# Transposing pairs of bf16 columns as 4-byte elements, and reading every second value as weights

## Chip, core and metric

The kernel runs on one core of one Trainium2 chip. The metric is device time in microseconds (us); lower is better. A run's time is that of the whole execution; the profile's span runs from the first to the last recorded instruction.

## What is computed

The reference is the forward pass and all gradients of two branches that share a layer-normalised input: segment-wise attention with a recurrent memory (A), and an MLP with a squared ReLU (B).

```python
xn = _layernorm(x)
out = x + A(xn, mem0, Wq, Wk, Wv, Wo) + B(xn, w1, b1, w2, b2)

# A: 64 segments of 32 rows, one after the other
mem = mem0                                  # 8 rows
for s in range(n_seg):
    h = concatenate([mem, xs], axis=1)      # 8 + 32 rows of 512
    q, k, v = h @ Wq, h @ Wk, h @ Wv        # 32 heads of 128
    p = softmax(where(mask, q @ k.T * scale, -1e9))
    o = (p @ v) @ Wo
    mem = o[:, :8]                          # goes into the next segment
    outs.append(o[:, 8:])
```

x is 2048 x 512 in bf16, F of the MLP is 1792. The outputs are the result and the gradients of x, mem0, Wq, Wk, Wv, Wo, w1, b1, w2 and b2. The memory makes the 64 segments a chain, forward in one direction and backward in the other.

## The kernel before

**Stages.** First the MLP and the layer norm (to 228 us of the span); then the 64 forward segments (to about 1290); a short turn of the weights (to about 1352); the 64 backward segments (to about 2516); and last the weight gradients of the attention as long runs of 512-column products (to the end). Four segments make a block of 128 rows. A step is one segment.

**Layout of a segment.** The 32 heads are laid out as 8 groups (index i) of 4 heads (index j, "JQ = 4"). In the natural layout (qN, oN, dN and so on, 128 x 1024) the partitions are 4 heads times 32 rows, and the columns are 8 groups times 128 features of a head. Products with Wo or with the turned Wq, Wk, Wv need the transposed layout (OT, dT, LT, qLT): features on the partitions, 32 rows as the columns of each weight. TensorE reads these as stationary weights of 128 x 32, four at a time in four column strips of the array, while the weight matrix streams past.

**The transposes.** `sq_T` (line 395) makes this layout without PSUM: for each half (four groups) one instruction of the VectorE (DVE) transposes 32 x 32 blocks. A block takes every fourth column of a head's 128 features (c is the column modulo 4), so that the 32 features a of one c end up on the partitions of that head's strip; the strip j and the index c together say which weight rows a product needs. Wo is loaded, and Wq, Wk, Wv are turned, in an order of rows to match (`turn`, `turn_o`). `sq_T` is called for oN to OT in each forward step (line 944), for oLN to qLT in `l_attn` (once a block), for dN2, dN1 and dN0 to dT2, dT1 and dT0 in each backward step (in `part`), and for dLN to LT0, LT1 and LT2 in `l_post` (once a block): 640 instructions in all.

**Who reads them.** `wo_part` (line 807) multiplies OT or qLT with Wo: 128 products of 128 columns, in four parts of 32; parts 0 and 1 need the first half of OT, parts 2 and 3 the second. `dh_part` (line 1110) multiplies dT or LT with the turned weights: 32 products of 512 columns, in four parts of 8; the three of a step add up in one PSUM bank.

**A forward step (`chain`, line 907).** Products for q and k; transposes on TensorE; scores; softmax on DVE and ScalarE (ACT); products for v; two DVE transposes of the probabilities (lines 938 and 939); products p v ("ps_o"); eviction to oN by ACT or DVE; `sq_T`; `wo_part` ("ps_RA"); the first eight rows go into the next step's input ("ps_mem", line 951).

**A backward step (`chain`, line 1236).** Products gO and their transposes; dP; the backward of the softmax, four DVE instructions one after the other (lines 1101 to 1106, result in the tile maskA); then three parts, each with a block-diagonal product ("ps_d"), an eviction to dN, `sq_T` and `dh_part`: part 2 needs only gO and P, parts 1 and 0 the softmax. After the last product of part 0 two evictions to R_A (half by ACT, half by DVE), small products ("ps_gm") and a copy into PA (line 1287) end the step.

**Work beside the chain.** Once a block, `l_proj` and `l_attn` (forward) and `l_pre` and `l_post` (backward) treat the block's 32 memory rows; the MLP's weight gradients ("ps_dw", `dw_unit`) fill the forward stage. In `l_pre` the tile dLN is computed (ps_dqL) and stored to S_GNL in DRAM; `l_post` of the block before reloads such a stored tile into the same dLN, transposes it to LT0, then evicts two more products (ps_dL) into dLN, each of which is transposed (LT1, LT2) and stored.

**What sets the order.** Every operation is given to a planner (`_Plan`) with an estimated cost per engine, what it reads and writes, and a priority. `run` simulates the engines with these costs and picks, step by step, the operation that can start first, or one of higher rank (its longest path to the end, from the same costs) that is about to be ready; a change of the shape of TensorE's tiles costs 2.0 us of rank in the backward stage (KEEP). An eviction may go to DVE or ACT, whichever ends it first by the estimates. The order found this way is the program's order on each engine, on the SP queue (loads and stores) and on the POOL queue. A cost changes nothing else: on the chip each engine takes its instructions in that order, and each waits for its own inputs.

Of the kernel before, what the change touches and what calls it, by code (L numbers as in the profile page):

```python
# [16 lines left out]
F32 = mybir.dt.float32  # L17
# [12 lines left out]
def pe(cost, shape):  # L30
    x = _PE(PE=cost)
    x.shape = shape
    return x
# [154 lines left out]
def kernel(  # L188
# [27 lines left out]
    nc = tc.nc  # L216
# [31 lines left out]
    JQ = 4  # L248
# [76 lines left out]
    def part_of(t, x, n):  # L325
        return t[x // n][:, x % n, :]
# [7 lines left out]
    def flat(t):  # L334
        return t[:].rearrange("p i e -> p (i e)")

    EV_F = {"DVE": 0.70, "ACT": 0.59}
    EV_B = {"DVE": 0.44, "ACT": 0.59}
    T_DMA = 0.42

    class Stage:
# [53 lines left out]
        def sq_T(self, src, sk, dst, dk, prio):  # L395

            for half in range(2):
                x = slice(4 * half, 4 * half + 4)
                self.plan.add({"DVE": 0.70}, lambda e, x=x: nc.vector.transpose(  # L399
                    dst[:, x, :, :], src[:, x, :].rearrange("p i (a c) -> p i c a", c=JQ)),  # L400
                    [(sk, half)], [(dk, half)], prio)

        def evict(self, out_f, bk, in_f, W, prio, cost, R=()):
# [3 lines left out]
        def proj(self, kind, nm, win, wkeys, Wt, col0, dst, prio):  # L407
            for half in range(2):
                bk = self.bank(kind, [P, 512], F32, "ps_" + nm)
                for dq in range(2):  # L410
                    def mm(e, half=half, dq=dq, bk=bk):
                        for dc in (2 * dq, 2 * dq + 1):
# [7 lines left out]
                self.evict(lambda half=half: dst[1][:, 4 * half:4 * half + 4, :].rearrange("p i e -> p (i e)"),  # L420
                           bk, lambda bk=bk: bk()[:], [(dst[0], half)], prio, EV_F)

# [18 lines left out]
        def diag(self, kind, nm, terms, rkeys, dst, prio):  # L441
            n = len(terms)
            for half in range(2):
                bk = self.bank(kind, [P, 512], F32, "ps_" + nm)

                def mm(e, half=half, bk=bk):
                    for k in range(4):
                        i = 4 * half + k
                        for x, (lf, rf, m) in enumerate(terms):
# [7 lines left out]
                self.evict(lambda half=half: dst[1][:, 4 * half:4 * half + 4, :].rearrange("p i e -> p (i e)"),  # L457
                           bk, lambda bk=bk: bk()[:], [(dst[0], half)], prio, EV_F)

# [21 lines left out]
    def wtf(t, h):  # L481
        return Wqkv[t][:, :, h * P:(h + 1) * P]
# [27 lines left out]
    with tc.tile_pool(name="p0", bufs=1) as p0, \  # L510
# [184 lines left out]
        for g in range(NRB):  # L695
            if g == 0:
# [12 lines left out]
                bk = sg.bank("B", [P, DC, RB], BF16, "ps_gT")  # L709
# [25 lines left out]
            if g < 6:  # L735
                for h in range(2):
                    x = 2 * g + h
                    t, dc = x // DC, x % DC
# [16 lines left out]
    with tc.tile_pool(name="fw", bufs=1) as fw, \  # L755
# [51 lines left out]
        def wo_part(kind, nm, OTt, ok, prio):  # L807
            bk = sg.bank(kind, [P, P], F32, "ps_R" + nm)
            for q in range(4):
                def mm(e, q=q):  # L810
                    for i in (2 * q, 2 * q + 1):
                        for j in range(JQ):
                            for jd in range(DC):
                                nc.tensor.matmul(  # L814
                                    bk()[32 * jd:32 * (jd + 1), :], lhsT=OTt[:, i, j, :],
                                    rhs=Wo[:, JQ * i + j, jd * P:(jd + 1) * P],
                                    start=(i == 0 and j == 0), stop=(i == NI - 1 and j == JQ - 1),
                                    tile_position=(0, 32 * jd),
                                )
                A(pe(0.54, "w"), mm, [(ok, q // 2), "WB"], [bk.key], prio)  # L820
            return bk
# [172 lines left out]
        def dw_unit(which, u):  # L994
# [16 lines left out]
            for x in range(2):  # L1011
                fc = 2 * u + x
                sg.evict(lambda: wt[:], bks[x], lambda x=x: bks[x]()[:], ["wt"] + ([("dw", u + FC // 2 * which)] if x else []), 1, EV_F)
                if which == 0:
# [39 lines left out]
    if True:  # L1054
# [55 lines left out]
        def dh_part(kind, nm, XT, xk, t, first, last, prio, bk=None):  # L1110
            if bk is None:
                bk = sg.bank(kind, [P, D], F32, "ps_dR" + nm)
            for q in range(4):
                def mm(e, q=q):
                    for i in (2 * q, 2 * q + 1):
                        for j in range(JQ):
                            nc.tensor.matmul(bk()[32 * j:32 * (j + 1), :], lhsT=XT[:, i, j, :],  # L1117
                                             rhs=wtf(t, JQ * i + j), start=(first and i == 0),
                                             stop=(last and i == NI - 1), tile_position=(0, 32 * j))
                A(pe(0.435, "w"), mm, [(xk, q // 2)] + [((t, "WT"), g) for g in range(4 * q, 4 * q + 4)], [bk.key], prio)  # L1120
            return bk
# [42 lines left out]
        def l_post(b):  # L1164
# [8 lines left out]
            for t, ly, lx, lk, big, pad, dst, dk, bn, pn in (parts if b else parts[::-1]):  # L1173
# [37 lines left out]
                for half in range(2):  # L1211
                    sg.evict(lambda half=half: dLN[:, 4 * half:4 * half + 4, :].rearrange("p i e -> p (i e)"), bks[half],
                             lambda half=half, bks=bks: bks[half]()[:], [("dLN", half)], 1, EV_F)
                sg.dma(lambda t=t: part_of(S_GNL[t], b, BPC), lambda: flat(dLN), both("dLN"), [("S_GNL", t, b)])
# [3 lines left out]
            for x, (t, L_) in enumerate(order):  # L1218
                bR = dh_part("f" if b else LKIND, "L", L_, "LT%d" % t, t, x == 0, x == 2, 1, bR)
            sg.evict(lambda: flat(btL), bR, lambda: bR()[:], ["btL"], 1, EV_F)  # L1220
            sg.dma(lambda: S_RL[b], lambda: flat(btL), ["btL"], [], cost=T_DMA + (b == 0), eng="SP" if b else "POOL")
# [14 lines left out]
        def chain(s):  # L1236
# [52 lines left out]
            else:  # L1289
                bm = sg.bank("c", [M, D], F32, "ps_dm0")  # L1290
                A(pe(0.9, "f"), lambda e: nc.tensor.matmul(bm()[:], lhsT=sel8[:], rhs=R_A[:], start=True, stop=True),
                  [("R_A", 0), ("R_A", 1)], [bm.key], 0)
                sg.evict(lambda: gNat[0:M, :], bm, lambda: bm()[:], ["gNat"], 0, EV_F)
                sg.dma(lambda: out2flat[:, :], lambda: gNat[0:M, :], ["gNat"], [])
# [25 lines left out]
        for b in range(TC - 1, -1, -1):  # L1320
            for v in range(SPB - 1, -1, -1):
                s = b * SPB + v
# [23 lines left out]
        for x in range(NRC // BPC):  # L1346
            c0 = (3, 2, 1, 0, 4)[x] * BPC
            src = S_HNA if c0 < TC else S_HNL
# [16 lines left out]
    with tc.tile_pool(name="p5b", bufs=1) as p5b, tc.tile_pool(name="p5e", bufs=1) as cs1, \  # L1365
# [60 lines left out]
        with tc.manual_schedule():  # L1426
            load_gn(0)
            for x in range(4 * JQ):
                t, j = (2, 1, 0, 3)[x // JQ], x % JQ
# [71 lines left out]
```

## Time and profile before

| | us |
|---|---|
| median of 3 runs (lowest to highest) | 3122.26 (3120.48 to 3124.76) |
| span of the profiled execution | 3097.7 |
| forward stage, 228 to 1290 us | 1062 |
| backward stage, 1352 to 2516 us | 1164 |
| TensorE (PE) busy in the span | 2792.6 |
| DVE busy in the span | 1538.8 |
| ACT busy in the span | 933.7 |

The page shows the span of the profiled execution; the launch around it is not in the span. A group of instructions is named by its line, engine and operation, output and input, with its count, busy time, the mean of one in ns, and the idle time of the engine ahead of it with what ended it. PEld is TensorE's loading of weights, which overlaps its products; "issue" is idle time in which nothing that the profile shows was waited for. Helpers have one line for all their calls: 318 is every eviction by ACT, 316 by DVE, 399 every `sq_T`, 361 most DMAs.

### The profile page before, as it was taken

The page shows a single profiled execution, that of the slowest core. Times are in us where ns is not written, and L with a number is a line of the kernel's source. Part 1 is how long each engine was busy: PE and PEld are TensorE (multiplying, and loading weights), DVE is VectorE, ACT ScalarE, POOL GpSimd, SP SyncE. Part 2 cuts the span into 40 slices and gives each one's busy share as a digit, 9 for nine tenths or more (in the row PEclk, how much of TensorE's full clock was granted, in tenths as well). Part 3 has the DMA queues.
Part 4 walks back from the last instruction along what each step waited for, and adds up shares of the span by engine and source line. Part 5 has one row for each costly group of instructions (what it writes and reads, how often), then busy time and mean ns, then how long its engine had stood idle before and what let it go on. Part 6 is the DMA issues. An engine that isn't in the chain of part 4 may idle for free.

```text
span 3097.7 us, 138545 instructions
## 1 busy us (share of the span) xinstructions
PE 2792.6 (90%) x62681; PEld 1629.5 (53%) x62847; DVE 1538.8 (50%) x3390; ACT 933.7 (30%) x1809; POOL 260.8 (8%) x434
## 2 busy tenths in 40 slices
PE   8998889898889898798888898889899889999999
PEld 6664555555555555564555555555555544444444
DVE  5544545555545455575555565565556521233322
ACT  4323434433434344342233333333333310000000
POOL 1110000000000000100000000000000001121111
PEclk9999999999999999999999999999999989999999
DMA  6647655566665563357677777777777669789861
GB/s 205 217 155 212 173 157 171 160 174 167 163 160 153 162 168 125 98 143 195 184 208 193 204 204 202 207 200 213 208 214 206 201 238 351 223 253 280 253 184 45
DMA packets 554918, 590.54 MB, mean 191 GB/s; under 512 B 250197, under 2 KB 355110, under 8 KB 552150
## 3 DMA queue, kind: packets, MB, share of 16 engines
q1 hardware_dynamic: 538758, 527.06, 59.8%
q0 software_dynamic: 15568, 54.61, 5.3%
q8 instruction: 491, 8.04, 1.2%
q14 instruction: 101, 0.83, 0.1%
HBM read 283.32 MB, written 262.68 MB: 176 GB/s over the span
## 4 chain that ended last, share of the span: by engine, by line
PE 67%; issue 10%; DVE 8%; DMA 8%; SPq 3%; ACT 2%; POOL 1%; ACTq 0%; POOLq 0%; DVEq 0%
PE ps_gw L1448 11%; PE ps_dRA L1117 9%; PE ps_d L451 6%; PE ps_RA L814 4%; PE ps_q L415 4%; PE ps_k L415 3%; PE ps_h L609 3%; PE ps_gO L415 3%; SPq L361 3%; PE ps_dRL L1117 3%; PE ps_v L415 2%; PE ps_dw L1009 2%; PE ps_gm L1284 2%; PE ps_o L451 2%; PE ps_gxb L637 2%
## 5 line engine op out<-in xcount | busy, mean ns | idle before, releaser
L1117 PE MATMUL ps_dRA<-WA,dT 128*32 128x512 bf16 x6144 | 376.6, 385 | 12.9 <-issue 10.4
L1448 PE MATMUL ps_gw<-WA,WB 128*128 128x512 bf16 x1505 | 330.7, 379 | 2.2 <-DVE gwo L316 0.6
L415 PEld LDWEIGHTS <-PA 128*32 128x32 bf16 x8192 | 207.5, 98 | 235.7 <-issue 29.8
L1448 PEld LDWEIGHTS <-WB 128*128 128x128 bf16 x1896 | 185.4, 98 | 225.0 <-issue 1.9
L399 DVE STREAM_TRANSPOSE dT<-dN 128x512 bf16<-128x512 bf16 x384 | 255.5, 692 | 90.7 <-ACT dN L318 89.4
L318 ACT CAST dN<-ps_d 128x512 bf16<-128x512 f32 x356 | 198.8, 588 | 292.0 <-PE ps_d L451 257.2
L1117 PEld LDWEIGHTS <-dT 128*32 128x32 bf16 x6144 | 158.0, 97 | 169.5 <-issue 26.5
L316 DVE CAST gwo<-ps_gw 128x512 bf16<-128x512 f32 x64 | 39.7, 683 | 399.5 <-PE ps_gw L1448 268.2
L814 PE MATMUL ps_RA<-WB,OT 128*32 128x128 bf16 x8192 | 139.3, 223 | 58.2 <-issue 41.9
L318 ACT CAST gwo<-ps_gw 128x512 bf16<-128x512 f32 x64 | 32.9, 599 | 515.3 <-PE ps_gw L1448 357.8
L316 DVE CAST kN<-ps_k 128x512 bf16<-128x512 f32 x117 | 80.9, 691 | 191.4 <-PE ps_k L415 188.4
L415 PE MATMUL ps_q<-WA,PA 128*32 128x512 bf16 x2048 | 160.9, 383 | 9.5 <-DVE PA L951 5.5
L814 PEld LDWEIGHTS <-OT 128*32 128x32 bf16 x8192 | 123.4, 99 | 78.9 <-issue 48.2
L415 PE MATMUL ps_k<-WA,PA 128*32 128x512 bf16 x2048 | 159.7, 380 | 1.6 <-issue 1.3
L451 PEld LDWEIGHTS <-PB 32*32 32x32 bf16 x8192 | 120.4, 93 | 72.6 <-issue 33.9
L415 PE MATMUL ps_gO<-WB,PA 128*32 128x512 bf16 x2048 | 139.5, 418 | 15.1 <-DVE PA L1287 14.9
L1227 POOL COPY bVT<-VR 128x1024 bf16<-128x1024 bf16 x64 | 66.6, 1041 | 959.1 <-PE ps_dP L1249 880.8
L318 ACT CAST qN<-ps_q 128x512 bf16<-128x512 f32 x119 | 69.6, 585 | 197.8 <-PE ps_q L415 194.7
L415 PE MATMUL ps_v<-WA,PA 128*32 128x512 bf16 x2048 | 128.1, 378 | 0.0
L1009 PE MATMUL ps_dw<-sx,anT 128*128 128x512 bf16 x358 | 108.0, 385 | 10.3 <-DMA sx<-in_grad_out_dram 6.6
L399 DVE STREAM_TRANSPOSE OT<-oN 128x512 bf16<-128x512 bf16 x128 | 83.8, 691 | 59.6 <-ACT oN L318 59.0
L1117 PE MATMUL ps_dRL<-WA,LT 128*32 128x512 bf16 x1536 | 111.2, 395 | 1.4 <-issue 1.0
(298 smaller groups left out, 4778.2 us busy)
## 6 DMA issues: line engine op xcount, KB each, us to landing
S_GN<-dN SPq DMA_DIRECT2D x192, 256.0 KB
WA<-S_GN SPq DMA_DIRECT2D x160, 256.0 KB
S_Q<-qN SPq DMA_DIRECT2D x64, 256.0 KB
S_K<-kN SPq DMA_DIRECT2D x64, 256.0 KB
S_V<-vN SPq DMA_DIRECT2D x64, 256.0 KB
S_ON<-oN SPq DMA_DIRECT2D x64, 256.0 KB
bqN<-S_Q SPq DMA_DIRECT2D x64, 256.0 KB
bkN<-S_K SPq DMA_DIRECT2D x64, 256.0 KB
```

Of the source, the lines that this page charges most:

```text
L316: nc.vector.tensor_copy(out, in_)
L318: nc.scalar.copy(out, in_)
L361: self.plan.add({eng: cost}, lambda e: q.dma_start(out_f(), in_f()), R, W, prio, lat)
L399: self.plan.add({"DVE": 0.70}, lambda e, x=x: nc.vector.transpose(dst[:, x, :, :], src[:, x, :].rearrange("p i (a c) -> p i c a", c=JQ)), ...
L415: nc.tensor.matmul(bk()[32 * j:32 * (j + 1), :], lhsT=win(dc), rhs=Wt(dc, c0), start=(dc == 0), stop=(dc == DC - 1), tile_position=(0, 32 ...
L451: nc.tensor.matmul(bk()[32 * j:32 * j + m, k * P:(k + 1) * P], lhsT=lf(j, i), rhs=rf(j, i), start=(k == 0 and x == 0), stop=(x == n - 1), ...
L609: nc.tensor.matmul(bk()[:, x, :], lhsT=Wt[:, dc, fc * P:(fc + 1) * P], rhs=In[:, dc, :], start=(dc == 0), stop=(dc == DC - 1), skip_group_ ...
L814: nc.tensor.matmul(bk()[32 * jd:32 * (jd + 1), :], lhsT=OTt[:, i, j, :], rhs=Wo[:, JQ * i + j, jd * P:(jd + 1) * P], start=(i == 0 and j = ...
L1009: nc.tensor.matmul(bks[x]()[:], lhsT=anT[x][:, c, :], rhs=sx[z][:], start=(c == 0), stop=(c == TC - 1))
L1117: nc.tensor.matmul(bk()[32 * j:32 * (j + 1), :], lhsT=XT[:, i, j, :], rhs=wtf(t, JQ * i + j), start=(first and i == 0), stop=(last and i = ...
L1227: A({"POOL": 1.0}, lambda e: nc.gpsimd.tensor_copy(VT[:, :, :, M:KA].rearrange("p i j r -> p (i j) r"), VR[:].rearrange("p i j r -> p (i j ...
L1448: nc.tensor.matmul(bks[n]()[:], lhsT=HNc[:, rc, dc * P:(dc + 1) * P], rhs=gns[y][:, hf * 512:(hf + 1) * 512], start=(y == 0), stop=(y == N ...
```

## The change

`sq_T` reads its source and writes its destination as 4-byte elements, each of which is two neighbouring bf16 columns. One instruction then handles 256 elements a partition instead of 512: 8 blocks of 32 x 32 instead of 16. A block takes every second pair of columns (u is the pair modulo 2). In the destination, a row's two values s = 0 and 1 of a pair now lie side by side, so the weight for column class k = 2u + s is every second value of a run of 64; the new helper `tq` gives that view, and `wo_part` and `dh_part` use it for their weights. The class k holds the same features as c did. The planner's cost for the transpose goes from 0.70 to 0.42.

```diff
+    def tq(t, i, k):
+        return t[:, i, :, :].rearrange("p c r -> p (c r)").rearrange("p (u r s) -> p u s r", u=2, s=2)[:, k // 2, k % 2, :]
+
@@ sq_T
-                self.plan.add({"DVE": 0.70}, lambda e, x=x: nc.vector.transpose(
-                    dst[:, x, :, :], src[:, x, :].rearrange("p i (a c) -> p i c a", c=JQ)),
+                self.plan.add({"DVE": 0.42}, lambda e, x=x: nc.vector.transpose(
+                    dst[:, x, :, :].rearrange("p i c r -> p (i c r)").bitcast(F32).rearrange("p (i u r) -> p i u r", u=2, r=32),
+                    src[:, x, :].rearrange("p i e -> p (i e)").bitcast(F32).rearrange("p (i a u) -> p i u a", a=32, u=2)),
                     [(sk, half)], [(dk, half)], prio)
@@ wo_part
-                                    bk()[32 * jd:32 * (jd + 1), :], lhsT=OTt[:, i, j, :],
+                                    bk()[32 * jd:32 * (jd + 1), :], lhsT=tq(OTt, i, j),
@@ dh_part
-                            nc.tensor.matmul(bk()[32 * j:32 * (j + 1), :], lhsT=XT[:, i, j, :],
+                            nc.tensor.matmul(bk()[32 * j:32 * (j + 1), :], lhsT=tq(XT, i, j),
```

## The prediction

> **What bounds the kernel now.** I read the page first: one line of busy times, then the groups of the line that the change rewrites.
>
> ```profile
> PE 2792.6 (90%) x62681; PEld 1629.5 (53%) x62847; DVE 1538.8 (50%) x3390; ACT 933.7 (30%) x1809; POOL 260.8 (8%) x434
> ...
> L399 DVE STREAM_TRANSPOSE dT<-dN 128x512 bf16<-128x512 bf16 x384 | 255.5, 692 | 90.7 <-ACT dN L318 89.4
> ...
> L399 DVE STREAM_TRANSPOSE OT<-oN 128x512 bf16<-128x512 bf16 x128 | 83.8, 691 | 59.6 <-ACT oN L318 59.0
> ```
>
> TensorE (PE) is busy 90%, VectorE (DVE) half. Line 399 runs 384 + 128 + 96 (LT) + 32 (qLT) = 640 times at 0.69 us. An engine half idle gains nothing by itself; what counts is who waits. So next the view of line 399 alone:
>
> ```profile
> who waited for it (us, times):
>   PEld L814: 32.0, 49
>   ACT dLN L318: 20.8, 11
>   PE ps_RA L814: 15.5, 19
>   POOL PB L1139: 15.1, 2
>   PEld L1117: 9.4, 35
> ```
>
> TensorE's weight loads wait for these transposes in 49 of the 64 forward steps (L814), on average 0.65 us; in the backward steps (L1117) hardly at all. The chain of waits agrees: its pieces on line 399, added up over the whole chain, are 23.5 us OT, 16.8 dT and 6.1 LT, 46.4 in all. The busy time by stretch gives the stages: forward 228 to 1290 us with 134 us of idle PE, backward 1352 to 2516 with 128.
>
> **The price of the parts.** No row shows a transpose of 4-byte elements. The nearest rows handle as many elements as the new instruction (256 a partition), in 2 bytes:
>
> ```profile
> L938 DVE STREAM_TRANSPOSE PB<-P 128x256 bf16<-128x256 bf16 x64 | 28.0, 437 | 0.0
> ...
> L939 DVE STREAM_TRANSPOSE PB<-PLp 128x256 bf16<-128x256 bf16 x64 | 25.7, 402 | 0.0
> ```
>
> I take 0.42, between the two, so 0.27 us less each and 173 us less DVE work. Bounds: 0.69, if a 4-byte element takes two passes (no gain), and 0.28, the quickest 256-element DVE row (L614, 285 ns).
>
> The weights with a step of 2: products of 512 columns run four at a time, 245 ns a group (L1117: 376.6 us for 6144), and hide four loads each. In wo_part (L814, 128 columns) the timeline shows 96 loads in 1.39 us, the pace of the products. The nearest row is the turning of WA (L312), which reads weights with a step of 4: 115 ns against 98 for the contiguous kN, and eight loads in 0.51 us against 0.45. Of these 0.06 us, 0.015 is latency; the rest is 5 ns per 128 columns, or 1.3 ns per load of 32. Times 10,240 loads of L814 that is 13 us at most. Eight of those transposes take 0.61 us against 0.62 for contiguous WB, so the pace of the products does not change: I take 0. [...]
>
> **Forward.** Of the 64 steps, the 16 with l_attn hold two transposes more and stall on "issue" before L814 (60.3 us in all, gaps where nothing is waited for); I count nothing there. In the other 48 OT's first half comes 0.27 us sooner: 13 us; the chain's share says 23.5 x 0.27/0.69 = 9. I take **-10** (bounds 0 and -18). Late next: ACT's eviction of oN, which the transposes themselves wait for (59.0 us).
>
> **Backward: the order changes.** The planner sorts instructions by estimated cost, and 0.70 became 0.42. The instruction order of the built changed kernel, against that of the one before, shows what follows. Before, nearly every step runs the products for dN0 in one piece ahead of the last dh_part products. In 30 of 62 steps of the changed kernel (3 before) dN0's first half comes early and its second half only after half of dT0's products, so that eviction, transpose and the last products stand in a row; and in 15 of them (2 before) nothing lies between dP and the products that wait for the whole softmax. The steps come in pairs, two of every block of four. DVE's other work, ACT's evictions, the SP queue's loads and the l_post products move with them: the reload of dLN now falls due a step later, and ACT's eviction of the next dLN, which waits for the store of the one before, stands ahead of ACT's R_A, the end of the step.
>
> One block of the kernel before happens to have this very order: the steps from 1478 us (a step runs from one copy of ps_gm into PA, L1287, to the next). Busy time by stretch, first its four steps, then four of a regular block:
>
> ```profile
> 1478.48:1498.05 19.57, 16.32 (x528) 10.35 (x532) 12.19 (x24) 5.35 (x10) 1.38 (x2) 0.91 0.45 136
> 1498.05:1521.33 23.28, 17.17 (x484) 10.81 (x476) 13.72 (x26) 5.45 (x10) 1.68 (x3) 0.90 0.97 256
> 1521.33:1540.43 19.10, 19.10 (x444) 9.95 (x446) 8.68 (x19) 4.28 (x8) 1.38 (x2) 0.85 0.55 166
> 1540.43:1555.70 15.27, 14.72 (x412) 8.43 (x412) 8.67 (x18) 4.86 (x9) 1.38 (x2) 1.00 0.88 197
> 2083.16:2103.03 19.87, 15.97 (x516) 10.01 (x516) 12.37 (x24) 6.99 (x13) 1.68 (x3) 1.00 0.67 175
> 2103.03:2121.64 18.61, 17.43 (x452) 11.12 (x456) 10.68 (x23) 5.87 (x11) 1.38 (x2) 0.91 0.82 250
> 2121.64:2137.70 16.06, 16.06 (x436) 9.15 (x435) 8.70 (x19) 4.95 (x9) 1.38 (x2) 1.00 0.78 207
> 2137.70:2154.00 16.30, 15.62 (x472) 9.46 (x464) 10.48 (x22) 5.53 (x10) 1.38 (x2) 1.00 0.70 208
> ```
>
> After the length come busy PE, PEld, DVE, ACT and POOL, then the granted clock. The odd block takes 77.25 us; the twelve regular blocks from 1571 to 2440 us average 72.4: **+4.85**. It also shows why:
>
> ```profile
> 1506.25 0.23 PE L451 MATMUL ps_d<-bqN,maskA 32*32 32x128 bf16 x4 [2.21 <-DVE maskA L1106]
> ...
> 1518.81 0.58 ACT L318 CAST dLN<-ps_dL 128x512 bf16<-128x512 f32 x1 [3.69 <-DMA S_GNL<-dLN]
> ```
>
> PE idles 2.2 us for the softmax, ACT 3.7 us for a store ahead of R_A, and the granted clock falls to 0.85 to 0.91 in three steps. The regular block loses clock in one; there DVE idles 3.0 us at 2100.8 for dLN's reload.
>
> What the shorter transposes give back in such a block, walked through its timeline: first odd step 0.2 (two of dT2 ahead of PB) + 0.28 (PE waits 0.55 for dT0) = 0.5; second 0.6 (five shorter transposes ahead of dLN let its store start some 1.2 earlier, but ACT now evicts both halves behind it, which takes 1.1 instead of 0.6); 0.3 each in the other two: 1.7. So 14 further blocks cost 14 x (4.85 - 1.7) = **+44**. The bounds: +18 more, as the odd block holds 1.3 us less work than a full one (16 gL products at 54 ns, eight transposes at 56), and -41 if its third step keeps the full clock (0.15 of 19.1 us = 2.9 a block).
>
> MLP, weight gradients and launch are untouched: 0. The sum: 3122 - 10 + 44 = **3156**, say 3155. The profiled span is 3097.7; 24.6 us of the median lie around it and stay.
>
> **Rivals.**
> (1) Faster: the odd block was slow by accident, and only the 46.4 us that line 399 holds of the chain shrink by 0.27/0.69: -18, 3104. For it: a single block, with DMA busy 97% in its second step. Against: the 2.2 us gaps follow from the order.
> (2) Faster, by the clock: were the dips not to come, the odd block would be shorter by 0.09 x 16.3 + 0.01 x 17.2 + 0.15 x 19.1 = 4.5 us, nearly the whole +4.85; 14 x (0.35 - 1.7) - 10 = -29, 3093. The trace speaks against it: the first odd step shows 0.91 with no gap above 2.2 us. The Trainium skill, TensorE: Matmul & The Clock Gate, Part 1, states that the clock halves only after an idle window of about 3.4 us; by that rule this case holds, and the row 0.91 disagrees.
> (3) The 4-byte transpose takes 0.69 like the old one: the change doesn't do what it says, the new order stays: 14 x 4.85 = +68, 3190.
> (4) Stepped weights cost 1.3 ns a load on L814: +13 on the forecast, 3168.
> (5) Gain and order cancel: 3122.
>
> **How the numbers follow.** Forecast 0.51 (alone 3130 to 3185), (1) 0.17, (2) 0.07, (3) 0.09, (4) 0.06, (5) 0.10. Measurement tells some 0.2% (6 us) from no change: faster 0.24, same 0.10, slower 0.66. The range 3100 to 3190 leaves out (2) and the upper half of (3).
>
> **What would show it.** Line 399 at 0.40 to 0.44 us (else 3). PEld's wait at L814 for OT near 20 instead of 32 us. Backward blocks near 75.5 us instead of 72.4, with PE gaps of 2 us before ps_d<-maskA, ACT dLN waiting for S_GNL, and granted clock under 0.95 in two or three steps of four. Backward blocks at 71 would make me wrong, by (1) or (2). L814's loads above 16 ns apiece would show (4).

## The result and the profile after

| | before | changed |
|---|---|---|
| median of 4 runs, us (lowest to highest) | 3121.37 (3100.27 to 3124.76) | 3161.7 (3148.22 to 3168.89) |
| ratio to before, 95% interval | | 1.0152 [1.0121, 1.0182] |
| span of the profiled execution, us | 3097.7 | 3161.9 |
| backward steps, first to last copy of ps_gm into PA, us | 1132.1 | 1185.5 |
| forward steps, first to last copy of ps_mem into PA, us | 1038.0 | 1054.4 |
| mean of 13 whole blocks (the second to the fourteenth of the backward stage), us | 72.62 | 77.26 |

The changed kernel is slower: by 40 us (1.3%) by the medians, by 1.52%, some 47 us, by the ratio of the runs. The 64 us between the two spans are 53.4 in the backward steps, 16.4 in the forward steps and -6 in the rest. The 16 in the forward steps do not belong to the change: the kernels below that have the forward order of before take 1045 to 1054 us there, too (e1, e4, e7, e8), and on a third chip the same order takes 1023.5 us (e12), so these steps vary by some 30 us between runs and chips. The profile of before is of a quick execution: the changed kernel's profiled run (3163.7) lies 1.8 us above its span, and by the same margin a span of 3097.7 belongs to a run of about 3099.5 us, 22 under the median and near the fourth of its runs (3100.27).

First the page and the groups of the changed kernel: busy times, then line 402, which is line 399 of before.

```profile
PE 2830.5 (90%) x62669; PEld 1647.3 (52%) x62847; DVE 1427.5 (45%) x3459; ACT 898.7 (28%) x1740; POOL 260.7 (8%) x434
...
L402 DVE STREAM_TRANSPOSE dT<-dN 128x256 f32<-128x256 f32 x384 | 163.0, 434 | 170.4 <-ACT dN L318 166.6
...
L402 DVE STREAM_TRANSPOSE OT<-oN 128x256 f32<-128x256 f32 x128 | 57.3, 448 | 52.9 <-ACT oN L318 49.8
```

The instruction does what was promised: 0.43 to 0.45 us instead of 0.69. DVE is busy 111 us less, and the kernel is slower.

Next the waits of TensorE within the backward stage (us in total, times, longest), of before and of the changed kernel, both from 1384 to 2515 us of the span (the changed kernel's last 55 us of backward steps are not in it):

```profile
PE ps_d L451 <- DVE maskA L1106: 17.1, 24, 2.2
...
PE ps_dL L1205 <- DMA ys<-S_PL: 9.7, 12, 1.7
```

```profile
PE ps_d L455 <- DVE maskA L1110: 54.5, 28, 3.0
PE ps_dL L1209 <- DMA ys<-S_PL: 36.4, 27, 2.6
```

Two waits grew: 37 us more for the softmax, which the prediction named, and 27 us more for ys, a load of `l_post`, which it did not. (In e1 below, which has the order of before, the wait for ys is 17.6 us, so a part of the 27 varies between runs.) Then busy time by stretch, for four steps of one changed block and the fourth step of the next (length; busy PE, PEld, DVE, ACT, POOL; granted clock; share of DMA busy; GB/s):

```profile
1532.59:1551.13 18.54, 16.27 (x436) 9.35 (x436) 7.35 (x18) 4.28 (x8) 1.38 (x2) 1.00 0.68 196
1551.13:1566.70 15.57, 15.54 (x428) 8.91 (x424) 7.80 (x20) 5.54 (x10) 1.38 (x2) 1.00 0.79 194
1566.70:1585.49 18.79, 15.96 (x536) 10.04 (x537) 11.80 (x26) 5.25 (x10) 1.38 (x2) 1.00 0.48 143
1585.49:1609.87 24.38, 19.04 (x492) 10.60 (x484) 10.15 (x25) 5.84 (x11) 1.63 (x3) 0.86 0.95 238
...
1660.06:1686.85 26.79, 20.12 (x492) 11.66 (x484) 10.34 (x24) 6.33 (x12) 1.88 (x3) 0.80 0.98 263
```

One step of four holds nearly the whole loss. On average over the fifteen blocks it takes 24.3 us at a DMA share of 0.94; the longest of the four in before takes 20.4 us, and no place there averages over 0.79 DMA. The other three together take 52.5 us, and 52.3 in before. The timeline of TensorE in such a step (1660.06 to 1686.85 us) shows what stands there:

```profile
1662.04 0.62 PE L1209 MATMUL ps_dL<-xs,ys 128*32 128x128 bf16 x32
...
1667.71 0.23 PE L455 MATMUL ps_d<-bqN,maskA 32*32 32x128 bf16 x4 [2.98 <-DVE maskA L1110]
...
1676.14 0.39 PE L1198 MATMUL ps_dL<-gLN,bPLL 32*32 32x128 bf16 x16
1676.46 0.23 PE L1209 MATMUL ps_dL<-xs,ys 128*32 128x128 bf16 x1
1678.26 0.23 PE L1209 MATMUL ps_dL<-xs,ys 128*32 128x128 bf16 x1 [1.57 <-DMA ys<-S_PL]
1680.54 0.82 PE L1209 MATMUL ps_dL<-xs,ys 128*32 128x128 bf16 x14 [2.05 <-DMA ys<-S_PL]
...
1682.23 1.92 PE L1121 MATMUL ps_dRA<-WA,dT 128*32 128x512 bf16 x16
```

`l_post` has two rounds of ps_dL that use the same tiles xs and ys: t = 1, then t = 2, with eight loads for each. In the changed kernel both rounds fall into this one step. The first ends at 1662.7; only then can the tiles be loaded again, and the second round, at 1676, finds ys not yet there. Behind the waiting products in PE's order stand the chain's last sixteen (line 1121), so the chain waits 3.6 us for a load that it does not need. In before the two rounds lie in two steps (in the regular block of the prediction at 2096.6 and at 2109 to 2112 us), and the second stands around dP and the softmax, where the chain is with DVE; there PE waits 0.57 us for ys:

```profile
2096.63 0.63 PE L1205 MATMUL ps_dL<-xs,ys 128*32 128x128 bf16 x32
...
2109.98 0.60 PE L1205 MATMUL ps_dL<-xs,ys 128*32 128x128 bf16 x14 [0.57 <-DMA ys<-S_PL]
```

The order of the SP queue, which issues the loads, has its part in this. The last loads of ys for the two second rounds above are issued here, first in the changed kernel, then in before:

```profile
1675.12 0.90 SPq L364 DMA_DIRECT2D ys<-S_PL  x2
```

```profile
2105.06 0.88 SPq L361 DMA_DIRECT2D ys<-S_PL  x2
```

The time between the two rounds is no shorter in the changed kernel (13.7 us on average of the 13 blocks, 11.6 in before). But its SP queue gets to the last ys only 12.8 us after the first round, among the chain's own loads and stores, and 0.9 us ahead of the products; in before it is 8.3 us after the one and 3.3 us ahead of the other.

### The profile page after: what moved, and what is told of

Its sections match the earlier page's. It is cut to its first block, busy times and chain, and to the rows that moved or that the text cites. A ratio compares the mean times of both kernels' runs of the same rounds, so it can differ in the third digit from the quotient of the medians.

```text
span 3161.9 us, 138714 instructions
## 1 busy us (share of the span) xinstructions
PE 2830.5 (90%) x62669; PEld 1647.3 (52%) x62847; DVE 1427.5 (45%) x3459; ACT 898.7 (28%) x1740; POOL 260.7 (8%) x434
## 5 line engine op out<-in xcount | busy, mean ns | idle before, releaser
L1121 PE MATMUL ps_dRA<-WA,dT 128*32 128x512 bf16 x6144 | 394.3, 403 | 21.3 <-issue 12.8
L402 DVE STREAM_TRANSPOSE dT<-dN 128x256 f32<-128x256 f32 x384 | 163.0, 434 | 170.4 <-ACT dN L318 166.6
L419 PE MATMUL ps_q<-WA,PA 128*32 128x512 bf16 x2048 | 168.9, 396 | 6.7 <-DVE PA L955 4.2
L455 PEld LDWEIGHTS <-PB 32*32 32x32 bf16 x8192 | 129.4, 96 | 76.0 <-issue 26.7
L419 PE MATMUL ps_k<-WA,PA 128*32 128x512 bf16 x2048 | 167.5, 392 | 0.6 <-DVE PA L955 0.3
L1231 POOL COPY bVT<-VR 128x1024 bf16<-128x1024 bf16 x64 | 66.9, 1045 | 882.6 <-PE ps_dP L1253 840.0
L419 PE MATMUL ps_gO<-WB,PA 128*32 128x512 bf16 x2048 | 127.7, 392 | 1.8 <-DVE PA L1291 0.9
L455 PE MATMUL ps_d<-bqN,maskA 32*32 32x128 bf16 x2048 | 71.5, 224 | 62.6 <-DVE maskA L1110 59.7
L1013 PE MATMUL ps_dw<-sx,anT 128*128 128x512 bf16 x346 | 109.0, 391 | 11.6 <-DMA sx<-in_grad_out_dram 6.0
```

The lines of the kernel that those rows point to most:

```text
L402: self.plan.add({"DVE": 0.42}, lambda e, x=x: nc.vector.transpose(dst[:, x, :, :].rearrange("p i c r -> p (i c r)").bitcast(F32).rearrange ...
L419: nc.tensor.matmul(bk()[32 * j:32 * (j + 1), :], lhsT=win(dc), rhs=Wt(dc, c0), start=(dc == 0), stop=(dc == DC - 1), tile_position=(0, 32 ...
L455: nc.tensor.matmul(bk()[32 * j:32 * j + m, k * P:(k + 1) * P], lhsT=lf(j, i), rhs=rf(j, i), start=(k == 0 and x == 0), stop=(x == n - 1), ...
L1013: nc.tensor.matmul(bks[x]()[:], lhsT=anT[x][:, c, :], rhs=sx[z][:], start=(c == 0), stop=(c == TC - 1))
L1121: nc.tensor.matmul(bk()[32 * j:32 * (j + 1), :], lhsT=tq(XT, i, j), rhs=wtf(t, JQ * i + j), start=(first and i == 0), stop=(last and i == ...
L1231: A({"POOL": 1.0}, lambda e: nc.gpsimd.tensor_copy(VT[:, :, :, M:KA].rearrange("p i j r -> p (i j) r"), VR[:].rearrange("p i j r -> p (i j ...
```

## The experiments

Each ratio is to the kernel before, on the same chip. The medians of before differ between chips (3112 us for e1 to e4, 3105 for e5 to e8, 3086 for e9 to e12), so ratios are compared, and stages and blocks within a batch. "Blocks" is the mean of the same 13 blocks, from the profile.

| | ratio, 95% | backward steps, us | blocks, us |
|---|---|---|---|
| changed kernel | 1.0152 [1.0121, 1.0182] | 1185.5 | 77.26 |
| e1 order of before | 0.9984 [0.9960, 1.0008] | 1129.4 | 72.34 |
| e2 new order, old transposes | 1.0220 [1.0194, 1.0247] | 1193.4 | 77.33 |
| e3 new order in the forward stage alone | 0.9983 [0.9963, 1.0003] | 1125.2 | 72.12 |
| e4 stepped weights alone | 1.0000 [0.9982, 1.0018] | 1122.7 | 72.20 |
| e5 new order, no loads | 0.9913 [0.9882, 0.9943] | 1106.6 | 70.94 |
| e6 new order, short softmax | 1.0185 [1.0148, 1.0222] | 1191.7 | 77.14 |
| e7 order of before, no loads | 0.9898 [0.9861, 0.9934] | 1088.5 | 69.68 |
| e8 order of before, short softmax | 0.9975 [0.9956, 0.9994] | 1129.2 | 72.19 |
| e9 new order, other tiles read | 1.0202 [1.0182, 1.0221] | 1192.7 | 77.49 |
| e10 loads said to land later | 1.0139 [1.0094, 1.0184] | 1169.4 | 75.96 |
| e11 cost 0.54 | 1.0190 [1.0161, 1.0219] | 1195.2 | 76.99 |
| e12 cost 0.70, KEEP 3.0 | 1.0052 [1.0031, 1.0073] | 1147.6 | 74.39 |

### Which part of the change costs: e1 to e4

Theory A: the loss is the order that the planner makes of the lower cost. Theory B, its rival: the new instructions cost time by themselves.

e1, in the changed kernel, and e2, in the kernel before:

```diff
-                self.plan.add({"DVE": 0.42}, lambda e, x=x: nc.vector.transpose(   # e1
+                self.plan.add({"DVE": 0.70}, lambda e, x=x: nc.vector.transpose(
-                self.plan.add({"DVE": 0.70}, lambda e, x=x: nc.vector.transpose(   # e2
+                self.plan.add({"DVE": 0.42}, lambda e, x=x: nc.vector.transpose(
```

> The changed kernel with the planner's cost of the transpose put back to 0.70, so that every engine has the order of before and only the instructions are new. Theory A (the loss is the order; the shorter transposes by themselves gain): 3095 to 3112 us, backward blocks of 71 to 73 us as before. Theory B (the new transposes or the stepped weights cost time by themselves): 3130 us or more, with the blocks above 74. If both parts are worth nothing: within 6 us of before.

> The kernel of before (2-byte transposes, contiguous weights) with only the planner's cost at 0.42, so in the order of the changed kernel. Theory A: at least as slow as the changed kernel, 3165 to 3200 us (the changed kernel's 3162 and up to 1.7 us more in each of 15 blocks and 10 in the forward stage); backward steps of 24 us or more once in a block. Theory B: within 10 us of before.

e3 gives the 0.42 to the forward stage alone (the backward plan is the one with KEEP):

```diff
-                self.plan.add({"DVE": 0.42}, lambda e, x=x: nc.vector.transpose(
+                self.plan.add({"DVE": 0.70 if self.plan.keep else 0.42}, lambda e, x=x: nc.vector.transpose(
```

> The changed kernel with cost 0.42 in the forward stage and 0.70 in the backward stage: forward order new, backward order that of before. Theory A with all of the loss in the backward order: equal to the kernel with cost 0.70 in both (e1) within 6 us. Rival: the 16 us that the changed kernel's profile shows longer in the forward stage come from its forward order too; then some 15 us slower than e1.

e4 is the kernel before with the two weight reads of the change:

```diff
-                                    bk()[32 * jd:32 * (jd + 1), :], lhsT=OTt[:, i, j, :],
+                                    bk()[32 * jd:32 * (jd + 1), :], lhsT=tq(OTt, i, j),
-                            nc.tensor.matmul(bk()[32 * j:32 * (j + 1), :], lhsT=XT[:, i, j, :],
+                            nc.tensor.matmul(bk()[32 * j:32 * (j + 1), :], lhsT=tq(XT, i, j),
```

> The kernel of before, with only the weights of the products of OT, qLT, dT and LT read with a step of 2 (2-byte transposes as before, so these products get the features in a wrong order). If the step costs nothing: within 6 us of before, weight loads of both products at 98 to 101 ns as before. If it costs 1.3 ns a load on the products with Wo: 13 us slower, about 3135 us; more if the backward products pay as well.

Theory A holds in all four. A number in the planner, 0.70 to 0.42, with not one instruction changed (e2), makes the kernel before slower by 2.2%; all new instructions without that number (e1) make it 0.16% faster, within the noise. The forward order (e3) and the stepped weights (e4) are worth nothing. Whether the shorter transposes bring something in the new order is not clear: e2 lies 0.7% above the changed kernel by its ratio, by the spans it is 6 us (3168.2 against 3161.9), and the blocks are equal.

Why is e1 not faster? The waits of PE in the forward stage, of e4 (old transposes) and of e1 (new ones), same chip and same order:

```profile
PE ps_RA L817 <- issue: 40.5, 36, 2.6
PE ps_oL L454 <- DMA VM<-S_VM: 19.9, 12, 3.5
PE ps_RA L817 <- DVE OT L402: 15.3, 19, 1.0
```

```profile
PE ps_RA L818 <- issue: 49.2, 39, 2.6
PE ps_oL L455 <- DMA VM<-S_VM: 25.1, 12, 3.8
...
PE ps_RA L818 <- DVE OT L402: 10.5, 18, 0.8
```

The wait for OT fell by 4.8 us, and the gaps in which nothing that the profile shows was waited for, ahead of the same products, grew by 8.7. The same gaps are 48.8 us in e7 and in e8 and 44.6 in e12, which have these transposes in this order, too, and 41.0 in before. The forward steps take 1048.8 us in e4 and 1053.6 in e1. The gain ran into the next wait.

### What in the new order costs: e5 to e8

Theory P is the prediction's: PE has nothing to do before the softmax is done. Theory Q is what the profile after suggests: the loads of `l_post` are bunched in one step, and PE's queue waits for them.

e5 leaves the loads of xs and ys out of 14 blocks, in the new order; e7 does the same in e1. `no_dma` plans the same operation and issues nothing, so all orders stay.

```diff
-                    sg.dma(lambda j=j, xx=xx: xx[j][:] if xx is xs else xx[j], lambda j=j, big=big: quad_rows(big, b, j),
+                    (sg.dma if b in (0, TC - 1) else no_dma)(lambda j=j, xx=xx: xx[j][:] if xx is xs else xx[j], lambda j=j, big=big: quad_rows(big, b, j),
...
-                    sg.dma(lambda j=j, yy=yy: yy[j], lambda j=j, pad=pad: quad_rows(pad, b, j),
+                    (sg.dma if b in (0, TC - 1) else no_dma)(lambda j=j, yy=yy: yy[j], lambda j=j, pad=pad: quad_rows(pad, b, j),
```

> The changed kernel in its own order; the loads of xs and ys of l_post are made only for the last and the first block, the 14 blocks between read what is there (16 loads a block left out, so the gradients of the memory rows are not the reference's). Theory Q (the new order bunches these loads into one step, where the PE queue then waits for ys: 36 us of idle PE against 10 before): 3115 to 3135 us, the long fourth step of the blocks down from 24.3 to 21 or less, DMA share there well under 0.95. Theory P (the loss is PE's wait for the softmax, with nothing before it to do): 3150 to 3165, the long step stays above 23.

> The control of e5: the same loads left out in the kernel of e1 (new transposes, order of before). Theory Q: 5 to 15 us under e1 (before's order waits 10 us for ys), so the two orders come 20 us or more nearer to each other. Theory P: as much gained as in e5.

e6 and e8 shorten the softmax in the changed kernel and in e1; inside `smax_bwd` every operand is cut to its first n groups:

```diff
-            smax_bwd("A", bk, KA, Pt[z], ("Pt", z), dS, "dS", 0, 0.51)
+            smax_bwd("A", bk, KA, Pt[z], ("Pt", z), dS, "dS", 0, 0.51, NI if s == NSEG - 1 else 1)
```

> The changed kernel in its own order; the four DVE instructions of the backward softmax of the chain work on one of eight groups of columns (in all steps but the first), so these gradients are not the reference's. Theory P: the idle PE ahead of ps_d<-maskA goes from 57 us to under 10, the time to 3095 to 3115 us. Theory Q: less than 25 us, since the wait for ys takes up what the softmax gives back in the fourth steps.

> The control of e6: the same short softmax in the kernel of e1. Theory P: 15 to 25 us under e1 (17.5 us of idle PE ahead of ps_d<-maskA, all gone), so that the two orders come 35 us or more nearer to each other. Theory Q: as much gained as in e6.

Theory P falls. The short softmax gains nothing in either order (1.0185 against 1.0152, 0.9975 against 0.9984). The waits of PE in the backward stage of e6 say where its time went:

```profile
PE ps_dL L1209 <- DMA ys<-S_PL: 43.7, 30, 3.9
PE ps_d L455 <- issue: 28.4, 29, 2.1
PE ps_d L455 <- DVE maskA L1110: 27.8, 26, 1.7
```

The wait for the softmax is 27 us shorter, the one on "issue" ahead of the same products 16 longer (12.7 before it), the one for ys 7 longer. It did not fall under 10 us as expected, so the test is not a full removal; but what it did remove was worth nothing.

Theory Q holds, more strongly than expected. Without the loads the two orders lie 0.15% apart (about 5 us, 0.9913 against 0.9898), with them 1.7% (about 52 us). By the profiles 18 of 56 us of the backward stage stay (1106.6 against 1088.5); the two profiled runs alone lie 13 us further apart than the medians (e5's 5 us above its own, e7's 8 below). The same block of e5 as above, by stretch:

```profile
1529.03:1544.70 15.67, 15.67 (x436) 9.25 (x436) 7.35 (x19) 4.19 (x8) 1.39 (x2) 1.00 0.51 162
1544.70:1560.26 15.56, 15.53 (x428) 8.96 (x424) 7.79 (x19) 5.55 (x10) 1.39 (x2) 1.00 0.78 195
1560.26:1579.64 19.38, 17.21 (x536) 10.38 (x537) 11.89 (x26) 5.36 (x10) 1.39 (x2) 0.91 0.46 139
1579.64:1598.86 19.22, 16.01 (x492) 9.62 (x484) 9.83 (x25) 6.03 (x11) 1.68 (x3) 1.00 0.86 212
```

The fourth step falls from 24.38 to 19.22 us, and its granted clock comes back from 0.86 to 1.00: of the 5.2 us, 3.0 are busy PE, which runs the same 492 products in 16.0 instead of 19.0 us. And the wait for the softmax is still there in e5, with all its size:

```profile
PE ps_d L455 <- DVE maskA L1110: 57.7, 31, 2.2
```

So that wait is no loss by itself: what the new order pays there it saves elsewhere (the waits of ps_gm for R_A, 22.5 us in before and 3.7 in the changed kernel, and of ps_gO for PA, 14.9 and 0.6).

### The wait or the traffic: e9 to e12

e9 was to keep the traffic and take the wait away, by letting the products of the second kind read tiles that the first kind (line 1198) has already read:

```diff
-                                    lhsT=yy[j][:, i * RL:(i + 1) * RL], rhs=xx[j][:, i * P:(i + 1) * P],
+                                    lhsT=(yy[j] if b in (0, TC - 1) else flat(ly))[:, i * RL:(i + 1) * RL], rhs=(xx[j] if b in (0, TC - 1) else flat(lx))[:, i * P:(i + 1) * P],
```

> The changed kernel in its own order with all of its loads; in the 14 blocks between the last and the first the products ps_dL read two tiles that are long there in place of xs and ys (so the gradients of the memory rows are not the reference's). It parts the two ways in which the loads of e5 can cost. Q1 (the products that wait for ys stand in PE's queue ahead of the last products of the chain): 3070 to 3105 us, as in e5. Q2 (the traffic by itself, which delays the chain's own loads in that step): 3130 us or more, the fourth step above 22 us. In between: both, in that share.

By its number this would be Q2, but the waits of PE show that the edit took one wait away and made another:

```profile
PE ps_dL L1209 <- DMA bqLN<-S_QL: 55.4, 13, 5.0
```

```profile
1648.04 1.04 PE L1209 MATMUL ps_dL<-bqLN,dSL 128*32 128x128 bf16 x32 [4.30 <-DMA bqLN<-S_QL]
```

The tile given to the first round (qLN) is loaded anew in that same step, and the products wait for that load, 4.3 us in each of 13 blocks, at the start of the step (from 1641.58 us in the line above); the second round, at its end, does not wait any more. So the test does not part the two ways. What it adds: the fourth step takes 24.3 us again, now with a DMA share of 0.82 instead of 0.94. Less the 4.3 us that is 20.0, near the 20.4 of before, with nearly all the traffic there: an estimate that speaks for the wait, not a run that shows it.

e10 tells the planner that the loads land later:

```diff
-                           [(bn, s) for s in range(b * SPB, b * SPB + SPB)], xk[j], lat=3.2)
+                           [(bn, s) for s in range(b * SPB, b * SPB + SPB)], xk[j], lat=6.0)
...
-                           yk[j], lat=3.0)
+                           yk[j], lat=6.0)
```

> The changed kernel with the planner told that the loads of xs and ys take 6 us to land (3.2 and 3.0 before). The PE order keeps its shape (dN0 in two halves in 31 steps, nothing between dP and ps_d1 in 15), but what the SP queue issues in the fullest step of a block falls from 5.5 MB on average to 4.7 (4.9 in the order of before). Theory Q: 3105 to 3140 us, idle PE for ys under 20 us instead of 36, the fourth step at 22 us or less. Theory P (the shape of the order costs): 3150 us or more.

e11 has 0.54 in place of the 0.42 in `sq_T`, and e12 has 0.70 there and `KEEP = 3.0`.

> The changed kernel with the planner's cost of the transpose at 0.54. No step runs dN0 in two halves; 14 have nothing between dP and ps_d1; the fullest step of a block issues 5.7 MB. Theory Q: 3145 to 3180 us, as slow as the changed kernel. If the late second half of dN0 were what costs (the prediction's first step): 3105 to 3130 us.

> The changed kernel with cost 0.70 as in e1 and the planner's price of a change of shape (KEEP) at 3.0 instead of 2.0. No step runs dN0 in two halves, one has nothing between dP and ps_d1, and the fullest step of a block issues 4.3 MB, the least of the orders built. Theory Q: 3070 to 3100 us, faster than both kernels. If neither the spread of the loads nor the shape of the order matters beyond e1: 3100 to 3115 us.

e10 went a part of the way in the profile (wait for ys 22.5 us in 14, fourth step 22.6 us, backward steps 16 us shorter than the changed kernel's) and by time cannot be told from the changed kernel (1.0139 against 1.0152). Its DMA share in the fourth step is 0.94, as in the changed kernel, so the spread of issues that I had counted was no spread on the chip. e11 came out as theory Q has it, as slow as the changed kernel without a single step that runs dN0 in two halves. e12 contradicts my forecast from megabytes issued in a step: the flattest order by that count is 0.5% slower than before, not faster. That count is no guide.

What does sort all the orders, seen only afterwards, is the place of the two rounds of ps_dL. In before, e1, e3, e4 and e8 they lie in two steps: blocks of 72.1 to 72.6 us. In the changed kernel, e2, e6, e9, e10, e11 and e12 they lie in one: 74.4 to 77.5. Three single cases fit. The odd block of the prediction, in the order of before, is the one block there with both rounds in one step: that step (1498.05 to 1521.33 us) takes 23.3 us in before and 23.0 to 26.8 in e1, e3, e4 and e8, but 20.4 in e7, without the loads. In e11 one block has the rounds spread over three steps (from 1552.07 us): its four steps take 71.7 us, those of the ten blocks after it 78.1 on average. And e12 has both rounds in one step, but its SP queue issues the last ys 6.5 us ahead of the products: PE waits for ys 4.0 us in all, and its blocks, at a DMA share of 0.81 in the longest step (e9: 0.82), are 3.1 us shorter than those of e9. No kernel with the two rounds apart by hand in the new order was run, so all this is observation.

## Why the prediction came out

It said 3155 us, 3100 to 3190, slower with 0.66; measured 3161.7. Its size is right, in part by luck, and its reason for the main term is not.

- **Transposes 0.42 us**: 0.43 to 0.45. Right; rival 3 falls.
- **Stepped weights 0**: right, e4 at 1.0000 (up to 6 us either way), its loads at 99 and 97 ns (OT and dT) as in before. Rival 4 (13 us) falls.
- **Forward -10**: not found. The waits for OT went as forecast (PEld 32.0 to 24.0 us, 20.1 in e1; 20 was named), but the gain ended in "issue" gaps. I had left these out for the 16 steps with `l_attn` only; ahead of the products of OT (ps_RA) in the other 48 they were 13 us in before and in e4 already, and are 19 in e1.
- **The order of the backward stage, +4.85 a block from the odd block**: right in size, almost to the digit: the odd block is 77.22 us by its four windows (77.25 in the text), the mean changed block 77.26. Against the 72.4 of the text that is +4.9; 13 whole blocks of before have 72.62, so +4.6.
- **The 1.7 us a block given back**: wrong. Blocks are 77.33 with the old transposes in the new order (e2) and 77.26 with the new. A likely reason, not tested, is that in the slow step the transposes have slack in front of a wait that ends by a load. So the backward term would have been +68 instead of +44. The stage shows 53.4: 13 blocks at 4.64 are 60, the first block is 2.6 shorter and the fifteenth 3.5 longer than in before, and the last two steps are 7.8 shorter. This is where luck came in: give-back and forward gain, 34 us that did not come, would have made +68 of the forecast's +34; the loss counted for edges where there is none (15) and the 6 us by which the rest of the kernel was shorter bring that back to +47, and the medians show +40.
- **Why the block is long**: wrong in the main. The prediction named the softmax (PE 2.2 us) and ACT's eviction that waits for the store. Both are there: 54.5 us in 28, and ACT dLN for S_GNL 60.6 us against 17.0. But what e6 took off the first was worth nothing, and the second goes to 1.0 us when the loads are left out (e5): it follows from the loads. What the prediction left out is those loads of xs and ys: without them the two orders lie 5 us apart instead of 52. They were in view, as the wrong piece of evidence: DMA busy 97% in the odd block's second step stood under rival 1 as a sign that the block was an accident. It is the step that holds both rounds of ps_dL, and the new order repeats that in every block. PE itself waits only 0.8 us for ys in that one step, so its length points at the traffic as well.
- **The clock**: the dips came, in two of the four places on average (0.95 and 0.86), so rival 2 falls. The row: in the step from 1660 us the granted clock is 0.80, and no idle stretch of PE is over 2.98 us. The Trainium skill, TensorE: Matmul & The Clock Gate, Part 1, has the clock halve after an idle window of about 3.4 us; this trace shows it lowered with shorter gaps, and the measurement decides. What e5 adds is that the dips get smaller without the loads: the clock of the fourth step is 0.86 on average with them and 0.92 without.
- **24.6 us around the span**: wrong. The execution that was profiled was itself about 22 us under the median, and some 2 us lie around the span. The forward stage was the quick part of it (1038 us, against 1045 to 1054 in e1, e4, e7 and e8), so the terms of the sum, which are differences within stages, were hardly touched.
- **Rival 1 (3104)** is what e1 tests in part: with the order of before, the gain is 0.4% at most, not the 0.6% worked out. Rival 5 (3122) falls: the interval of the ratio leaves out 1.

Open: how much of the step is the wait in PE's order, how much the traffic that delays stores and the chain's own loads, and how much the lower clock that comes with both. e5 takes all of it away at once, e9 did not part them, and e12 differs from e9 in more than the wait. A hand-made separation of the two rounds in the new order was not tried, nor an SP queue with the loads of ys further ahead.

## What to carry to other kernels

When a cost that a planner reads is changed, the order is the change: run the new instructions in the old order and the old instructions in the new order before believing either part. Where an odd block of the old trace already has the new order, its length can be a good price (here it was), but its reason must be read from all of its columns, the DMA share too. What the traces suggest, and no run tested: put products that wait for a load behind the recurrent chain's products, and issue that load well ahead of them (0.9 us here, 3.3 in the kernel before).

## What the runs showed of the hardware

- A DVE transpose of 256 4-byte elements a partition takes 419 to 448 ns (means of the four groups), against 402 and 437 for 256 elements of 2 bytes and 691 for 512: the number of elements counts, and twice the bytes cost little.
- Weights of 32 columns read with a step of 2 load as fast as contiguous ones: 99 ns (OT) and 97 ns (dT) on average, in e4 and in before.
- DMA traffic that a kernel can well carry on average (0.71 busy over the backward stage of the changed kernel, 0.73 in before) goes with a loss of some 50 us when 5.9 of a block's 14.7 MB fall into one step of four (at most 4.1 of 14.6 on average in before). How much of the loss the traffic itself makes is open.
- The granted clock fell with idle gaps of TensorE under 3 us: 0.80 over the step from 1660 us, whose longest gap is 2.98 us.
